# FFN products and sums of squares in two 64-column halves of the array, with a new order table

## The chip, the cores and the metric

The kernel runs on one core of one Trainium2 chip. The metric is the device time of one execution in microseconds (us). TensorE (PE in the profile) multiplies: it holds a block of weights in its array and streams another operand through it into a bank of PSUM. VectorE (DVE), ScalarE (ACT) and GpSimd (POOL) do the elementwise work, and SyncE (SP) issues transfers. Before the change three runs took 1124.65, 1126.27 and 1127.68 us; the median is 1126.27 us.

## The reference

Attention with a threshold below each row's maximum, over 8 batches of 8 heads with 576 positions of 64 elements, and behind it a feed-forward network (FFN) on 4,608 tokens of 512 features with 2,048 hidden ones:

```python
scores = scale * np.matmul(q, k.transpose(0, 1, 3, 2))
thresh = np.max(scores, axis=-1, keepdims=True) - tau
scores = np.where(scores >= thresh, scores, -1000000000.0)
scores = scores - np.max(scores, axis=-1, keepdims=True)
attn = np.exp(scores)
attn = attn / (np.sum(attn, axis=-1, keepdims=True) + 1e-09)
attn_out = np.matmul(attn, v)
...
x = np.ascontiguousarray(attn_out.transpose(0, 2, 1, 3)).reshape(B * S, H * D)
h = x @ w_in
g = np.where(h >= 1, h, np.where(h <= -1, 0.0, (h + 1) ** 2 / 4.0))
return g @ w_out
```

## The kernel before

Every operand of a large product is kept as two float16 parts, a high and a low one, and each product is made of three: high by high, high by low, low by high. Scales are powers of two that come from sums of squares.

The attention is cut by batch, pair of heads and a stretch of 256 or 320 rows (all of batch 0's in pieces of 128, 128 and 320). One *visit* makes two score tiles `s` of 128 rows by 576 (`products`, line 958 of the profile). A head has 64 elements, so these products use 64 of the array's rows, and two of them lie in the two row halves; in a tail visit both rows and columns are halved. A tile then goes through the softmax: VectorE finds the extreme (L1011), ScalarE takes the exponential (L1018), VectorE masks and sums (L1032), GpSimd normalises (L1050), ScalarE and GpSimd split into two parts `hl` (L1055, L1058), and a transposing DMA brings them into `eT`. Then `av` (L1156) multiplies with `v`. It gives 64 columns for each of the two heads of a pair, so it issues two products in turn, one into partitions 0 to 63 of a PSUM bank and one into 64 to 127; each uses 64 of the array's columns. The result becomes `x`, the FFN's input.

The FFN takes tokens in groups of 256 (or 128). `ffn1` (L1225) makes 24 products of 256 columns (48 of 128) into one bank `ph`; ScalarE and VectorE work out the gate (L1231 to L1248) and leave it in `ga`, `gb` or in a freed piece of the weights `WI`, `WO`; `ffn2` (L1270) makes 6 products (or 12) of 512 columns into the one bank `acc`, which ScalarE copies out (`evict`, L1288) when all parts of 128 tokens are in. Up to the change `ffn1`, `ffn2` and the small products with which sums of squares are added over partitions (L546 and L610) all use the whole array of 128 by 128.

So TensorE works in four layouts: the whole array (128*128 in the profile), two column halves (128*64), two row halves (64*128), and both (64*64).

Which engine does what in which order is written down. Each step is an operation of a `Plan`, with the engine, a cost and the buffers it takes. The list `ORDER` gives the sequence in which a planner places the operations; it works out a start time for each by their costs, and the steps are then issued sorted by these. An operation has a `mode` for its layout, and the planner adds `TURN`, 0.097 us, where the mode on TensorE differs from the one before. Small strings choose variants: `CONV` and `SIGN` for the conversion of the weights, `PAIR` for whether a visit's two tiles are one step, `TILE` for a softmax variant, `FSCALE` for the engine that works out a batch's scale factors (L920 to L926). In gaps of the plan's first 200 us, products with `ones` (L1304) keep TensorE active.

Of the kernel before, what the change touches and what calls it, by code (L numbers as in the profile page):

```python
# [18 lines left out]
P = 128  # L19
# [6 lines left out]
CONV = {"i": "GGMGPGGPPPGPMPQP", "o": "QAPADPPAPDPDDADD"}  # L26

SIGN = {"i": "ANANAAANNNNNNANA", "o": "AAANAAAAANAANAAD"}
PAIR = "SSJSJSJJSJSJJJJSSJJJJJJJJJJJJJJJJJJJJJJJJJJJJJJJJJJJJJJJJJJJJJJJJJJJJJJJJJJJJJJJJJJJJJJJJJJJJJJJJJJJJJJJJJJJJJJJJJJJJJJJJJJJJJJJJJJJJJJJJJJJJJJJ"
# [214 lines left out]
]  # L244
ESC = 2.0 ** 15

TILE = {0: "T", 1: "T", 71: "S", 272: "S"}
FSCALE = "GVVGVGGV"
EPS = 1e-9

# [15 lines left out]
class Plan:  # L266
# [38 lines left out]
    def order(self):  # L305
# [5 lines left out]
        for o in (self.ops[n] for n in ORDER):  # L311
# [10 lines left out]
            if o.eng == "PE":  # L322
                mode = o.mode
# [20 lines left out]
def attn_ffn_kernel(ctx: ExitStack, tc: tile.TileContext, qT, kT, vT, tau, w_in, w_out, out):  # L344
# [87 lines left out]
    def ap(b, arr):  # L432
        return arr[b.slot]
# [926 lines left out]
```

## Time and profile before

| | before |
|---|---|
| median of 3 runs (lowest to highest), us | 1126.27 (1124.65 to 1127.68) |
| the profiled execution, us | 1124.36 |
| its span, us | 1122.6 |
| mean granted clock of TensorE | 0.994 |
| HBM read, written | 45.09 MB, 9.44 MB |

The span runs from the first to the last instruction that was profiled. Busy times count an engine's own instructions; a product's row lasts until its result is out, which is longer than the distance to the next one. The distance between two rows' starts in the timeline is therefore the better measure of what a group of products takes.

### The profile page before, as it was taken

The numbers are of one execution on the slowest core, as the hardware profiler recorded it, in microseconds if no ns is written. First come the engines' busy times: TensorE is split into PE (matmuls) and PEld (weight loads), VectorE is DVE, ScalarE is ACT, GpSimd is POOL, SyncE is SP. The second block draws the span as 40 slices with busy tenths as digits, with TensorE's granted clock in tenths as the row PEclk, the third lists the DMA queues.
The fourth block names the chain that finished last, engine by engine and source line by source line (L and its number), as shares of the span: only waits on it lengthen the run. The fifth ranks groups of instructions, "written<-read, shape, count | busy, mean of one in ns | idle before, by whom it ended". The sixth has DMA issues, their size and how long they took to land.

```text
span 1122.6 us, 28192 instructions
## 1 busy us (share of the span) xinstructions
PE 1084.0 (97%) x10251; PEld 731.1 (65%) x10251; DVE 887.5 (79%) x2677; ACT 868.2 (77%) x1675; POOL 789.4 (70%) x912
## 2 busy tenths in 40 slices
PE   8789989999999999999999999999999999999998
PEld 7557647666766666666667666666676666766774
DVE  5899988998888887788879887788788797886331
ACT  7899768798788887788788798678788776776442
POOL 5999998787658986788768886676668885655000
PEclk9899999999999999999999999999999999999999
DMA  9797696868776985678666875757657667546000
GB/s 350 299 248 118 135 190 129 151 127 147 129 144 135 167 178 99 116 143 185 138 112 134 161 151 122 125 100 157 152 119 119 120 122 126 103 100 115 12 20 19
DMA packets 418011, 154.68 MB, mean 138 GB/s; under 512 B 396880, under 2 KB 396880, under 8 KB 417872
## 3 DMA queue, kind: packets, MB, share of 16 engines
q1 hardware_dynamic: 417872, 152.88, 66.7%
q8 instruction: 80, 1.31, 0.5%
q14 instruction: 59, 0.48, 0.2%
HBM read 45.09 MB, written 9.44 MB: 49 GB/s over the span
## 4 chain that ended last, share of the span: by engine, by line
PE 69%; DVE 9%; POOL 9%; ACT 4%; DMA 4%; issue 4%; SPq 0%; POOLq 0%; DVEq 0%; ACTq 0%
PE ph L1225 26%; PE acc L1270 25%; PE ph L1156 8%; PE s L958 8%; DMA eT<-hl 4%; POOL hl L1058 3%; DVE s L1011 2%; POOL e L1050 2%; DVE e L1032 2%; ACT hl L1055 1%; PE ph L1304 1%; ACT e L1018 1%; DVE ph L1238 1%; POOL raw L566 1%; PE s L660 1%
## 5 line engine op out<-in xcount | busy, mean ns | idle before, releaser
L1058 POOL TENSOR_TENSOR hl<-e,hl 128x576 f16<-128x576 f32 x284 | 364.1, 1290 | 91.3 <-ACT hl L1055 86.6
L1225 PE MATMUL ph<-x,WI 128*128 128x256 f16 (+1 forms) x4032 | 401.1, 258 | 2.4 <-DVE x L1168 0.8
L1225 PEld LDWEIGHTS <-WI 128*128 128x128 f16 x4032 | 343.7, 98 | 60.1 <-issue 16.4
L1050 POOL TENSOR_SCALAR e<-e,sm 128x576 f32<-128x576 f32 x284 | 219.9, 779 | 108.7 <-DVE sm L1042 80.4
L1011 DVE TENSOR_SCALAR_CACHE_REDUCE s<-s,pc 128x576 f32<-128x576 f32 x288 | 229.5, 819 | 49.2 <-PE s L958 46.3
L1032 DVE SCALAR_TENSOR_TENSOR e<-s,sm,e 128x578 f32<-128x578 f32 x284 | 229.1, 816 | 42.7 <-ACT e L1018 34.2
L1055 ACT ACTIVATE hl<-e 128x576 f16<-128x576 f32 x284 | 192.1, 681 | 84.2 <-POOL e L1050 67.3
L1018 ACT ACTIVATE e<-s,sm 128x576 f32<-128x576 f32 x288 | 209.6, 739 | 37.9 <-DVE s L1011 27.9
L1270 PE MATMUL acc<-WO,ga 128*128 128x512 f16 x864 | 202.2, 379 | 0.7 <-ACT ob L1288 0.4
L1238 DVE SCALAR_TENSOR_TENSOR ph<-ph,fcs,asq 128x512 f32<-128x512 f32 (+1 forms) x160 | 111.8, 700 | 66.7 <-ACT asq L1234 65.7
L958 PE MATMUL s<-kk,qq 64*128 64x288 f16 (+1 forms) x1920 | 141.5, 285 | 6.9 <-DVE e L1032 4.0
L1231 ACT ACTIVATE asq<-ph,fcs 128x512 f32<-128x512 f32 (+1 forms) x160 | 115.8, 736 | 37.6 <-PE ph L1225 36.1
L1270 PEld LDWEIGHTS <-ga 128*128 128x128 f16 x864 | 80.1, 98 | 93.1 <-issue 10.6
L1156 PE MATMUL ph<-eT,vst 128*64 128x320 f16 (+2 forms) x1928 | 123.3, 280 | 6.2 <-DMA eT<-hl 4.7
L958 PEld LDWEIGHTS <-qq 64*128 64x128 f16 (+1 forms) x1920 | 81.0, 96 | 65.1 <-issue 47.3
L1156 PEld LDWEIGHTS <-vst 128*64 128x64 f16 x1928 | 98.5, 110 | 34.4 <-issue 24.6
L1243 ACT ACTIVATE ga<-ph,fcs 128x256 f16<-128x256 f32 (+1 forms) x160 | 70.2, 450 | 29.6 <-DVE ph L1238 24.4
L1234 ACT ACTIVATE asq<-asq 128x512 f32<-128x512 f32 x144 | 90.5, 630 | 2.0
L1248 DVE SCALAR_TENSOR_TENSOR ga<-ph,fcs,ga 128x256 f16<-128x256 f32 (+1 forms) x160 | 70.9, 452 | 22.2 <-ACT WO L1243 7.4
L1270 PE MATMUL acc<-WO,gb 128*128 128x512 f16 x300 | 71.9, 379 | 0.0
L1270 PE MATMUL acc<-WO,WI 128*128 128x512 f16 x300 | 71.7, 379 | 0.0
L1270 PE MATMUL acc<-WO 128*128 128x512 f16 x264 | 63.4, 379 | 1.9 <-ACT ob L1288 1.9
(186 smaller groups left out, 1136.5 us busy)
## 6 DMA issues: line engine op xcount, KB each, us to landing
raw<-in_v_dram SPq DMA_DIRECT2D x32, 288.0 KB, 3.4
raw<-in_q_dram SPq DMA_DIRECT2D x32, 288.0 KB, 3.5
raw<-in_k_dram SPq DMA_DIRECT2D x32, 288.0 KB, 3.5
WO<-in_moe_w_in_dram SPq DMA_DIRECT2D x16, 512.0 KB, 8.5
out_dram<-ob SPq DMA_DIRECT2D x32, 256.0 KB, 2.5
x<-in_moe_w_out_dram SPq DMA_DIRECT2D x10, 512.0 KB, 6.8
eT<-hl SPq DMA_TRANSPOSE x286, 3.4
WO<-in_moe_w_out_dram SPq DMA_DIRECT2D x4, 512.0 KB, 6.1
```

What stands on the lines that cost most here:

```text
L958: T.matmul(ap(sb, s_ps)[r, f, :SH], ap(qb, qq)[h, ql, c : c + r.stop - r.start], ap(kb, kk)[h, kl, f * SH : (f + 1) * SH], start=ql == kl ...
L1011: V.tensor_scalar(sv(), sv(), c[:, 24 + v : 25 + v], None, ALU.mult, ALU.min, accum_out=t[:, 0:1])
L1018: A.activation(ev(), sv(), AF.Exp, bias=ap(m, sm)[:, 0:1], scale=-1.0)
L1032: V.scalar_tensor_tensor(ev(SH + 1), sv(SH + 1), t[:, 2:3], ev(SH + 1), ALU.is_le, ALU.mult, accum_out=t[:, 3:4])
L1050: G.tensor_scalar(ev(), ev(), ap(m, sm)[:, 5:6], ESC, ALU.mult, ALU.mult)
L1055: A.activation(part2(0), ev(), AF.Copy)
L1058: G.tensor_tensor(part2(w), ev(), part2(0), ALU.subtract)
L1156: T.matmul(o[hd * D : (hd + 1) * D, :n], vt[:, k, hd * D : (hd + 1) * D], t[:, kb, (hd ^ p % 2) * n : ((hd ^ p % 2) + 1) * n], start=m == ...
L1225: T.matmul(h[:, i], WTh["i"][:, u, wl * 512 + c * P : wl * 512 + (c + 1) * P], x[:, cc, xl, c0 : c0 + n].rearrange("p (t n) -> p t n", n=P ...
L1231: A.activation(tv()[:, :, c], hv()[:, :, c], AF.Relu, bias=fcs[:, b, 2, q : q + 1], scale=fcs[:, b, 3, q : q + 1])
L1238: V.scalar_tensor_tensor(hv()[:, :, c], hv()[:, :, c], fcs[:, b, 0, q : q + 1], tv()[:, :, c], ALU.max, ALU.min)
L1270: T.matmul(ap(ab, accs), gv(h, gl)[:, x], WTh["o"][:, fc + i, wl * 512 : (wl + 1) * 512], start=fc + i == 0 and m == 0, stop=not left[0] a ...
```

## The change

A function `columns` issues a product as two products of 64 weight columns each, the first into partitions 0 to 63 of the result and the second into 64 to 127, or as one whole product where `halves` is false. The FFN-1 of groups of 256 tokens, all of FFN-2 and the sums of squares go through it; the FFN-1 of 128 tokens stays whole. Their mode is a new one, 4, which stands for "either". `layouts` walks TensorE's operations in order and decides for each of mode 4: it keeps the layout of the last operation with a mode of its own if that is the whole array or the column halves; behind a layout of row halves it takes that of the next operation with a mode of its own, if that is the whole array or the column halves, and otherwise the column halves. `turned` is the same rule in the planner. The planned costs of the sums of squares are lower.

```diff
-CONV = {"i": "GGMGPGGPPPGPMPQP", "o": "QAPADPPAPDPDDADD"}
-
-SIGN = {"i": "ANANAAANNNNNNANA", "o": "AAANAAAAANAANAAD"}
+CONV = {"i": "GGMGPGGPPPGPMPQP", "o": "PAPADPPAPDPDDADD"}
+
+SIGN = {"i": "ANNNAAANNNNNNANA", "o": "AAANAAAAANAANAAD"}
...
 ORDER = [
-    0, 58, 56, 60, 54, 623, 633, 638, 4, 57, 628, 1, 5, 59, 2, 61, 658, 55, 648, 62, 63, 625, 653, 64, 624, 80, 626, 635, 643, 634, 75, 81, 636, 640,
...
+    0, 54, 58, 59, 56, 57, 60, 623, 633, 638, 1, 4, 628, 5, 2, 55, 658, 61, 648, 653, 625, 643, 62, 63, 64, 900, 80, 624, 626, 627, 634, 75, 635, 636,
...
-TILE = {0: "T", 1: "T", 71: "S", 272: "S"}
-FSCALE = "GVVGVGGV"
+TILE = {0: "T", 1: "T", 71: "S", 214: "S", 287: "S"}
+FSCALE = "GVGGGGGV"
...
+    def turned(self, at, to):
+
+        if to == 4:
+            return (False, at) if at in (0, 1, 4) else (True, 4)
+        return at != to and not (at == 4 and to < 2), to
+
+    def layouts(self, order):
+
+        at, after = 0, {}
+        seq = [o for o in order if o.eng == "PE"]
+        for o in reversed(seq):
+            after[o.n] = at
+            if o.mode != 4:
+                at = o.mode
+        at = 0
+        for o in seq:
+            if o.mode != 4:
+                at = o.mode
+            elif at > 1:
+                at = after[o.n] if after[o.n] < 2 else 1
+            o.layout = at
...
+    def columns(out, lhsT, rhs, halves=True, **flags):
+
+        for x in (slice(0, D), slice(D, P)) if halves else (slice(0, P),):
+            T.matmul(out[x], lhsT[:, x], rhs, **flags)
...
-                T.matmul(o[:, 2 * v : 2 * v + 2], sel[:, 2 + p % 2 if v == 2 else v], c, start=True, stop=True)
-
-        ps = plan.op("PE", 0.25, sums, [sq, sk], take=[sb], uses=[cb])
+                columns(o[:, 2 * v : 2 * v + 2], sel[:, 2 + p % 2 if v == 2 else v], c, ps.layout, start=True, stop=True)
+
+        ps = plan.op("PE", 0.18 if b else 0.09, sums, [sq, sk], take=[sb], uses=[cb], mode=4)
...
-                            T.matmul(h[:, i], WTh["i"][:, u, wl * 512 + c * P : wl * 512 + (c + 1) * P],
-                                     x[:, cc, xl, c0 : c0 + n].rearrange("p (t n) -> p t n", n=P), start=m == 0, stop=m == 3 * NCC - 1)
+                            columns(h[:, i], WTh["i"][:, u, wl * 512 + c * P : wl * 512 + (c + 1) * P],
+                                    x[:, cc, xl, c0 : c0 + n].rearrange("p (t n) -> p t n", n=P), k == 2 and me[0].layout, start=m == 0, stop=m == 3 * NCC - 1)
...
-                            T.matmul(ap(ab, accs), gv(h, gl)[:, x], WTh["o"][:, fc + i, wl * 512 : (wl + 1) * 512],
-                                     start=fc + i == 0 and m == 0, stop=not left[0] and i == k - 1 and m == 2)
+                            columns(ap(ab, accs), gv(h, gl)[:, x], WTh["o"][:, fc + i, wl * 512 : (wl + 1) * 512], me[0].layout,
+                                    start=fc + i == 0 and m == 0, stop=not left[0] and i == k - 1 and m == 2)
```

How this moves instructions is seen best on TensorE. In its built order before, around the end of an attention step a little before the middle of the program (`vst` is `v`, `eT` the transposed weights of attention; the last number is partitions by columns of the result):

```order
L1156 LDWEIGHTS vst_85
L1156 MATMUL ph_65<-eT_97,vst_85 64x256
L1225 LDWEIGHTS WI
L1225 MATMUL ph_64<-x_104,WI 128x2x128
L1225 LDWEIGHTS WI
L1225 MATMUL ph_64<-x_104,WI 128x2x128
```

And after, the start of the same attention step on TensorE, with what stands ahead of it:

```order
L461 LDWEIGHTS WI
L461 MATMUL ph_63<-x_104,WI 64x2x128
L461 LDWEIGHTS WI
L461 MATMUL ph_63<-x_104,WI 64x2x128
L1184 LDWEIGHTS vst_85
L1184 MATMUL ph_65<-eT_97,vst_85 64x256
```

Before, the step comes from scores and goes on to FFN-1 in the whole array; after, FFN-1 in halves of 64 columns stands ahead of it, and FFN-2 in halves behind it. Every half is an instruction of its own with its own weight load: TensorE's program has 29,250 rows where it had 20,346.

The second place, on TensorE, is where `acc` passes from one block of 128 tokens to the next, near 487 us of the profile before. In the order before (`ga` and `WO` hold gates, `sel` and `pc` are those of the sums of squares):

```order
L1270 LDWEIGHTS ga_108
L1270 MATMUL acc<-WO,ga_108 128x512
L546 LDWEIGHTS sel
L546 MATMUL ph_64<-pc_118,sel 128x2
L546 LDWEIGHTS sel
L546 MATMUL ph_64<-pc_118,sel 128x2
L546 LDWEIGHTS sel
L546 MATMUL ph_64<-pc_118,sel 128x2
L1270 LDWEIGHTS WO
L1270 MATMUL acc<-WO 128x512
```

And after, the same passing on TensorE, from the last product of the old block on:

```order
L461 LDWEIGHTS ga_108
L461 MATMUL acc<-WO,ga_108 64x512
L1184 LDWEIGHTS vst_87
L1184 MATMUL ph_63<-eT_96,vst_87 64x320
L1184 LDWEIGHTS vst_87
L1184 MATMUL ph_63<-eT_96,vst_87 64x320
```

Before, three small products lie between the last product into `acc` and the first of the next block; after, the 28 products of an attention step lie there.

The third place is ScalarE at the same passing, before (L1288 copies `acc` out):

```order
L1234 ACTIVATE asq_99<-asq_99 128x512
L1055 ACTIVATE hl_94<-e_92 128x576
L1288 ACTIVATE ob_100<-acc,scs 128x512
L1018 ACTIVATE e_91<-s_62,sm_120 128x2x288
L572 ACTIVATE kk_79<-raw_75 128x576
```

And ScalarE there after (L1321 is the same copy):

```order
L1083 ACTIVATE hl_94<-e_90 128x576
L1262 ACTIVATE asq_98<-asq_98 128x512
L1046 ACTIVATE e_91<-s_62,sm_121 128x2x288
L1321 ACTIVATE ob_100<-acc,scs 128x512
L1046 ACTIVATE e_92<-s_61,sm_122 128x2x288
```

The copy now stands behind an exponential as well, and the rest is exchanged among neighbours.

More of the change, by code (lines that the diff above doesn't have):

```diff
@@ L24 @@
 WIDE = 1
-CONV = {"i": "GGMGPGGPPPGPMPQP", "o": "QAPADPPAPDPDDADD"}
-SIGN = {"i": "ANANAAANNNNNNANA", "o": "AAANAAAAANAANAAD"}
-PAIR = "SSJSJSJJSJSJJJJSSJJJJJJJJJJJJJJJJJJJJJJJJJJJJJJJJJJJJJJJJJJJJJJJJJJJJJJJJJJJJJJJJJJJJJJJJJJJJJJJJJJJJJJJJJJJJJJJJJJJJJJJJJJJJJJJJJJJJJJJJJJJJJJJ"
+CONV = {"i": "GGMGPGGPPPGPMPQP", "o": "PAPADPPAPDPDDADD"}
+SIGN = {"i": "ANNNAAANNNNNNANA", "o": "AAANAAAAANAANAAD"}
+PAIR = "JSJSSSJJSJSJSJJSJJJJJJJJJJJJJJJJJJJJJJJJJJJJJJJJJJJJJJJJJJJJJJJJJJJJJJJJJJJJJJJJJJJJJJJJJJJJJJJJJJJJJJJJJJJJJJJJJJJJJJJJJJJJJJJJJJJJJJJJJJJJJJJJ"
 QHOW = "DDPDPPDPPPDPPPPPPPPPPPPPPDDPPPPP"
@@ L320, in order @@
                 b.since = t
-            end = idle[o.eng] = t + o.cost + (self.TURN if o.eng == "PE" and o.mode != mode else 0.0)
+            end = idle[o.eng] = t + o.cost
             if o.eng == "PE":
-                mode = o.mode
+                turn, mode = self.turned(mode, o.mode)
+                end = idle[o.eng] = end + self.TURN * turn
             if o.work:
@@ L609, in sums @@
         def sums():
-            T.matmul(stat(sb.slot, NPAIR), ones, cut(vssq[:, b, :]), start=True, stop=True)
-        ps = plan.op("PE", 0.1, sums, squares + [c_op], take=[sb])
+            columns(stat(sb.slot, NPAIR), ones, cut(vssq[:, b, :]), ps.layout, start=True, stop=True)
+        ps = plan.op("PE", 0.06 if b else 0.03, sums, squares + [c_op], take=[sb], mode=4)
         s = scs[:, b, :]
@@ L1214, in gv, with ffn1 @@
                 return (ga, gb)[h][qs[h].slot].rearrange("p (l k n) -> p l k n", l=2, n=P)[:, l]
-            def ffn1(hv=hv, g=g, fc=fc, c0=c0, n=n, k=k, q=q):
+            def ffn1(me, hv=hv, g=g, fc=fc, c0=c0, n=n, k=k, q=q):
                 h = hv().rearrange("p (t k) n -> p k t n", k=k)
@@ L1251, in attn_ffn_kernel @@
             wo = [wlo["o", x] for x in range(fc, fc + k)]
-            o = plan.op("PE", 12 * k * (n / 2400 + 0.0027), ffn1, xdone[g, c0] + xdone.get((g, c0 + n - P), []) + wi, take=[hb, qs[1]], uses=[xbuf[g]])
+            me = []
+            o = plan.op("PE", 12 * k * (n / 2400 + 0.0027), partial(ffn1, me), xdone[g, c0] + xdone.get((g, c0 + n - P), []) + wi, take=[hb, qs[1]], uses=[xbuf[g]],
+                        mode=4 if k == 2 else 0)
+            me.append(o)
             o = plan.op("ACT", 0.7 + 0.295 * (m - 1), relu, [o] + [fscale[b] for b in bs], take=[tb], uses=[hb])
@@ L1263, in attn_ffn_kernel, with ffn2 @@
             for fc, qs, gv, need in steps:
-                def ffn2(gv=gv, ab=ab, fc=fc, t0=t0, k=k, left=left):
+                def ffn2(me, gv=gv, ab=ab, fc=fc, t0=t0, k=k, left=left):
                     left[0] -= 1
@@ L1269, in ffn2 @@
                         for gl, wl in ((0, 0), (0, 1), (1, 0)):
-                            T.matmul(ap(ab, accs), gv(h, gl)[:, x], WTh["o"][:, fc + i, wl * 512 : (wl + 1) * 512],
-                                     start=fc + i == 0 and m == 0, stop=not left[0] and i == k - 1 and m == 2)
+                            columns(ap(ab, accs), gv(h, gl)[:, x], WTh["o"][:, fc + i, wl * 512 : (wl + 1) * 512], me[0].layout,
+                                    start=fc + i == 0 and m == 0, stop=not left[0] and i == k - 1 and m == 2)
                             m += 1
-                o.append(plan.op("PE", 3 * k * 0.216, ffn2, need, take=[ab] if fc == 0 else [], uses=[*(qs if k == 4 else [qs[t0 // P]]), ab], behind=head))
+                me = []
+                o.append(plan.op("PE", 3 * k * 0.216, partial(ffn2, me), need, take=[ab] if fc == 0 else [], uses=[*(qs if k == 4 else [qs[t0 // P]]), ab], behind=head, mode=4))
+                me.append(o[-1])
                 head = o[0]
@@ L1324, in attn_ffn_kernel @@
         order = plan.order()
+        plan.layouts(order)
         left = gaps(order)
```

406 rows, old and new, of the table ORDER are left out of this document.

## The prediction

> **What bounds the kernel now.** I read the page first, then the table of stretches, then TensorE's timeline. The page's engine rows (busy time, share, instructions) and its chain of work, followed back from the end:
>
> ```profile
> PE 1084.0 (97%) x10251; PEld 731.1 (65%) x10251; DVE 887.5 (79%) x2677; ACT 868.2 (77%) x1675; POOL 789.4 (70%) x912
> ...
> PE 69%; DVE 9%; POOL 9%; ACT 4%; DMA 4%; issue 4%; SPq 0%; POOLq 0%; DVEq 0%; ACTq 0%
> ```
>
> TensorE is busy 97% and carries 69% of the chain. The table of stretches says where the other 3% lie (length, then busy time of PE, PEld, DVE, ACT and POOL, the granted clock, the DMA share, GB/s):
>
> ```profile
> 0.00:100.00 100.00, 81.97 (x1015) 63.09 (x1016) 81.12 (x263) 88.22 (x174) 82.04 (x144) 0.95 0.89 272
> 100.00:200.00 100.00, 92.53 (x940) 61.55 (x938) 90.20 (x266) 78.69 (x151) 91.42 (x98) 1.00 0.80 149
> 200.00:500.00 300.00, 294.81 (x2735) 196.99 (x2735) 253.62 (x773) 244.51 (x477) 228.65 (x252) 0.99 0.74 139
> 500.00:800.00 300.00, 299.64 (x2769) 200.95 (x2768) 248.65 (x747) 239.70 (x462) 224.08 (x248) 1.00 0.70 138
> ```
>
> The first 200 us leave 25.5 us idle; from 500 to 800 the idle time is 0.36 us. So after the start the time is the sum of what TensorE executes, and a nanosecond saved there is a nanosecond of the end. But "busy" hides something, which the timeline shows by the distance from start to start (start, busy time, instructions):
>
> ```profile
> 611.73 0.91 PE L958 MATMUL s<-kk,qq 64*128 64x288 f16 x12
> 612.57 1.47 PE L1270 MATMUL acc<-WO 128*128 128x512 f16 x6
> 613.88 1.46 PE L1270 MATMUL acc<-WO,gb 128*128 128x512 f16 x6
> 615.17 0.22 PE L546 MATMUL ph<-pc,sel 128*128 128x2 bf16 x3
> 615.25 2.78 PE L1225 MATMUL ph<-x,WI 128*128 128x256 f16 x24
> 617.87 2.75 PE L1270 MATMUL acc<-WO,gb 128*128 128x512 f16 x12
> 620.46 1.46 PE L1270 MATMUL acc<-WO,WI 128*128 128x512 f16 x6
> 621.85 0.91 PE L958 MATMUL s<-kk,qq 64*128 64x288 f16 x12
> 622.69 2.76 PE L1270 MATMUL acc<-WO,WI 128*128 128x512 f16 x12
> 625.38 2.09 PE L1156 MATMUL ph<-eT,vst 128*64 128x320 f16 x28
> 627.40 0.93 PE L958 MATMUL s<-kk,qq 64*64 64x288 f16 x24
> 628.27 1.47 PE L1270 MATMUL acc<-WO,ga 128*128 128x512 f16 x6
> 629.57 1.46 PE L1270 MATMUL acc<-WO,WI 128*128 128x512 f16 x6
> ```
>
> Twelve FFN-2 products followed by more of their own shape take 617.87 to 620.46, 2.59 us; twelve followed by attention products in the 128*64 shape take 622.69 to 625.38, 2.69. Six take 1.29 before sums (613.88) and 1.39 before scores (620.46). Each change of layout (the shape behind the tile names) costs 0.095 us or so, with no wait in it.
>
> **Part 1, the changes of layout.** Walking TensorE's built order and counting the places where the layout of neighbouring products differs gives 374 before and 323 after. The 298 that enter or leave a layout of 64 rows (scores) stay 298: halves have 128 rows, and a score visit still lies between two changes. Those between whole array and 64 columns fall from 76 to 25: 51 x 0.095 = **-4.85 us**. All of it is on the path, since TensorE waits for nothing there.
>
> The entry into a layout has a small cost of its own. Two groups give it, and give the pace of half-width products too:
>
> ```profile
> 601.30 1.72 PE L1156 MATMUL ph<-eT,vst 128*64 128x256 f16 x28
> 602.95 1.47 PE L1270 MATMUL acc<-WO,ga 128*128 128x512 f16 x6
> ...
> 834.47 3.25 PE L1156 MATMUL ph<-eT,vst 128*64 128x256 f16 x56
> ...
> 1044.56 8.02 PE L1225 MATMUL ph<-x,WI 128*128 128x256 f16 x72
> ...
> 1055.01 2.78 PE L1225 MATMUL ph<-x,WI 128*128 128x256 f16 x24
> ```
>
> The 28 half-width products above stand 1.65 us until the next group; less 0.095 and less 14 pairs at 0.1093 (below) 0.025 is left for the entry. Into the whole array it is 0.01 (612.57 to 613.88 is 1.31 for six products, where 1.30 is usual). Stretches of half-width work rise from 65 to 137, those of whole-array work fall from 161 to 38: 72 x 0.025 - 123 x 0.01 = **+0.6 us**.
>
> **Part 2, 8,760 half-width FFN products in place of 4,380 whole ones.** 2,880 FFN-1 products of 256 columns and 1,500 of the 1,728 FFN-2 products are issued as two halves of 64 columns, one behind the other, into the two halves of one bank. Attention already works so, and the four rows above give its pace: 28 more products take 3.25 - 1.72 = 1.53 us, so a pair takes 109.3 ns; 48 more whole products take 8.02 - 2.78 = 5.24 us, 109.2 each. A pair of halves costs what one whole product costs: **0 us**. The 512-column pair isn't in the trace; at 320 columns a group of 28 stands 2.02 us (625.38 to 627.40), less 0.095 and 0.025 is 136 ns a pair, and 320/512 of FFN-2's 216 ns (2.59 us / 12) is 135. The other end: if the 0.025 of an entry were spread over its 14 pairs, each pair would carry 1.8 ns, 4,380 x 1.8 = +7.9 us. I take 0, since the longer row decides between the two readings, and keep +7.9 for the range. The whole gain of part 1 is 1.0 ns a pair; nothing below 0 is to be had, as the columns streamed stay the same.
>
> Each half needs its own weight load. The page has for the two kinds:
>
> ```profile
> L1225 PEld LDWEIGHTS <-WI 128*128 128x128 f16 x4032 | 343.7, 98 | 60.1 <-issue 16.4
> ...
> L1156 PEld LDWEIGHTS <-vst 128*64 128x64 f16 x1928 | 98.5, 110 | 34.4 <-issue 24.6
> ```
>
> A half load takes 110 ns, a whole one 98, and yet the pair above keeps 109.3: loads go on behind products. The Trainium skill, "TensorEngine Tiling (Array Packing)", Restrictions, says that column tiling switches fast weight load off, a rule against this change; the trace agrees that half a load isn't shorter (110 against 98), and not that it shows in the pace. By the rule alone, with loads in the open, the sum would end far above the time before (third rival).
>
> **Part 3, sums of squares (L546, L610).** 26 of the 32 groups of three tiny products become six halves. Three take 0.08 us (615.17 to 615.25). If halves run side by side as attention's do, nothing is added; one after the other, 26 x 0.08 = +2.1 us. Nearest is attention's row: **0**, the other end kept.
>
> **Part 4, the new order.** It mostly keeps the neighbourhoods; work on the other engines is the same but for a few conversions. One wait is visibly taken on. TensorE and ScalarE around it:
>
> ```profile
> 484.82 2.76 PE L1270 MATMUL acc<-WO,ga 128*128 128x512 f16 x12
> 487.42 0.22 PE L546 MATMUL ph<-pc,sel 128*128 128x2 bf16 x3
> 489.55 1.46 PE L1270 MATMUL acc<-WO 128*128 128x512 f16 x6 [1.91 <-ACT ob L1288]
> 490.93 2.09 PE L1156 MATMUL ph<-eT,vst 128*64 128x320 f16 x28
> 492.96 0.91 PE L958 MATMUL s<-kk,qq 64*128 64x288 f16 x12
> ...
> 487.73 0.62 ACT L1234 ACTIVATE asq<-asq 128x512 f32<-128x512 f32 x1
> 488.25 0.67 ACT L1055 ACTIVATE hl<-e 128x576 f16<-128x576 f32 x1
> 488.82 0.68 ACT L1288 ACTIVATE ob<-acc,scs 128x512 f32<-128x512 f32 x1
> ```
>
> The one accumulator must be copied out (L1288) before the next tokens' FFN-2 may start, and the copy stands behind two activations. TensorE has 0.08 us of sums to fill 2.13 us. In the new order attention's 28 products (2.03 us, 490.93 to 492.96) stand there instead: **-1.9 us**. What is late next: if the copy is later still, 0.1 us or so. Elsewhere a handover gets narrower: one near 220 us has 1.1 us of TensorE work between where it had 2.6. A copy takes 0.68 plus its queue; I set +0.3 (0 to +1.0). Two of the four small chains of scale factors that VectorE worked out go to GpSimd. It is busy 70%, and no row has TensorE waiting for these: 0.
>
> All waits of TensorE after 200 us, of which I count no others as gone (ten rows, 8.2 us together):
>
> ```profile
> PE ph L1156 <- DMA eT<-hl: 2.2, 2, 1.6
> PE acc L1270 <- ACT ob L1288: 1.9, 1, 1.9
> PE s L958 <- DVE e L1032: 1.5, 4, 0.5
> ...
> PE ph L1156 <- issue: 0.3, 1, 0.3
> ...
> PE ph L1225 <- DVE gb L1248: 0.2, 1, 0.2
> ```
>
> **Sum:** -4.85 + 0.6 + 0 + 0 - 1.9 + 0.3 = **-5.9 us**. The profiled execution took 1124.36 us (span 1122.6 and 1.8 around it): 1118.5. It lies 1.9 us below the median of the runs, 1126.27, from which the sum gives 1120.4. I take the middle, **1119.4**.
>
> **Rivals.**
> *New waits eat it.* The order was dealt anew, and a step that was just in time may be late. For it: softmax steps hold two score buffers, and VectorE is 85% busy from 200 to 500 (253.62 of 300). Against it: the neighbourhoods barely differ. Three waits of the size of the longest DMA wait, 1.6 us, make +4.8: 1124, the same within measurement.
> *The halves don't save the change.* If going from an FFN half to an attention half costs as much as a change of layout, only parts 1's +0.6 and part 4 remain: 1124.3. Against it: inside attention's rows the two halves alternate at full pace.
> *Loads in the open.* Here the price starts at 12 ns a pair (110 - 98): 4,380 x 12 = 53 us, 1172. Only the 56-product row, whose halves have different moving data, speaks against it; FFN halves share theirs. It decides from 1.0 ns a pair on.
> *The instruction stream, slower.* TensorE's program grows from 20,346 rows to 29,250. The queues of the page:
>
> ```profile
> q1 hardware_dynamic: 417872, 152.88, 66.7%
> q8 instruction: 80, 1.31, 0.5%
> ```
>
> 1.31 MB over 2 x 10,251 is 64 bytes each: q8 feeds TensorE, and gets 115 packets where it had 80, beside traffic that keeps the DMA engines 67% busy. If packets come late by the 0.3 us of the one "issue" wait, 31 of them undo 5.9 us and put the kernel 0.3% above; at 75 late ones +22.5: 1142. Place: stretches of FFN-1 halves, four instructions in 109 ns. Against it: attention runs at this rate, if only for 3 us at a time.
>
> **How the numbers follow.** A measurement of this kernel tells about 0.3% (3.4 us) from no change: below 1122.9 is faster, above 1129.6 slower. My forecast with the smaller mishaps has 0.64; new waits 0.24, a twelfth of it beyond 1129.6; halves that save nothing 0.04; the stream 0.06; open loads 0.02. Faster 0.64; same 0.22 + 0.04 = 0.26; slower 0.02 + 0.06 + 0.02 = 0.10. The range reaches down to 1112, where half of the remaining waits (3 us) and a sixth of the first 200 us' idle time go too, and up to 1128, which takes in part 2's +7.9 (1127.3) and the new waits.
>
> **What would show it.** FFN-1 groups in halves with 2.62 us from start to start for 24 pairs, and 1.30 for six FFN-2 pairs, show part 2 right; 2.67 or more shows the surcharge. FFN halves followed by attention without 0.09 us extra show part 1. The wait for L1288's successor near 485 us should be gone. "issue" in TensorE's waits beyond 1 us would show the stream. I am wrong if the waits after 200 us exceed 11 us, or if the first 200 us get longer by 3.

## The result, and the profile after

| | before | after |
|---|---|---|
| median (lowest to highest), us | 1125.46 (1122.65 to 1127.68), 4 runs | 1112.17 (1111.71 to 1114.32), 4 runs |
| the profiled execution, us | 1124.36 | 1114.32 |
| its span, us; granted clock | 1122.6; 0.994 | 1112.5; 0.991 |

The changed kernel takes 0.9887 of the time of the kernel before (95% interval 0.986 to 0.9913): 13.3 us less, where 5.9 were forecast from the sum (6.9 from the median then shown). The sign is right, the size half of what came, and the time is just inside the range's lower end.

The page after, engine rows (busy time, share of the span, instructions) and the chain by engine:

```profile
PE 1080.0 (97%) x14703; PEld 793.3 (71%) x14703; DVE 898.6 (81%) x2668; ACT 871.3 (78%) x1675; POOL 789.5 (71%) x921
...
PE 77%; DVE 8%; ACT 4%; DMA 4%; POOL 3%; issue 2%; SPq 0%; DVEq 0%; ACTq 0%; POOLq 0%
```

TensorE still carries the chain, with 77% of it instead of 69%. It was busy for 4.0 us less, while the span shrank by 10.1: most of what came is idle time. Stretches of the changed kernel (length, then busy time of PE, PEld, DVE, ACT and POOL, granted clock, DMA share, GB/s):

```profile
0.00:100.00 100.00, 81.67 (x951) 62.09 (x952) 79.16 (x257) 84.29 (x168) 79.19 (x143) 0.91 0.90 269
100.00:200.00 100.00, 95.45 (x1258) 68.95 (x1259) 93.56 (x274) 81.71 (x155) 94.14 (x102) 1.00 0.81 150
200.00:500.00 300.00, 297.45 (x4233) 220.62 (x4227) 260.32 (x779) 252.57 (x488) 235.84 (x264) 1.00 0.79 142
500.00:800.00 300.00, 297.60 (x4154) 217.62 (x4148) 252.40 (x745) 240.34 (x460) 219.94 (x244) 1.00 0.75 139
```

The first 200 us leave 22.9 us idle (25.5 before). TensorE's timeline (start, busy time) shows the halves:

```profile
608.60 2.79 PE L461 MATMUL ph<-x,WI 128*64 128x256 f16 x48
611.22 1.46 PE L461 MATMUL acc<-WO,WI 128*64 128x512 f16 x12
612.52 1.46 PE L461 MATMUL acc<-WO 128*64 128x512 f16 x12
613.81 1.46 PE L461 MATMUL acc<-WO,gb 128*64 128x512 f16 x12
615.21 1.21 PE L986 MATMUL s<-kk,qq 64*128 64x288 f16 x12
...
1029.92 2.07 PE L1184 MATMUL ph<-eT,vst 128*64 128x320 f16 x28
1031.82 2.76 PE L461 MATMUL acc<-WO,ga 128*64 128x512 f16 x24
```

From start to start, 24 pairs of FFN-1 take 2.62 us and six of FFN-2 1.30 or 1.29, and the six ahead of scores 1.40, one change of layout more. Attention's 28 products pass into FFN-2 in halves after 1.90 us; into the whole array it was 2.02. Both are as forecast, so the missing 7 us lie elsewhere.

TensorE's waits after 200 us show where to look: what waited, for whom, total us, times, longest. The kernel before in a second profiled execution (`e8_before_again` below):

```profile
PE ph L1156 <- DMA eT<-hl: 2.7, 2, 1.4
PE acc L1270 <- ACT ob L1288: 1.8, 1, 1.8
PE s L958 <- DVE e L1032: 1.3, 3, 0.5
PE ph L546 <- DVE pc L553: 0.7, 1, 0.7
```

and the changed kernel:

```profile
PE ph L1184 <- DMA eT<-hl: 2.7, 4, 1.0
PE ph L1184 <- DVE e L1060: 1.6, 1, 1.6
PE ph L1184 <- issue: 0.4, 1, 0.4
PE ph L461 <- DVE WI L1276: 0.2, 1, 0.2
```

In the kernel before the longest waits come back in both executions at the same places, at 417, 487 and 868 us, 8.2 and 7.7 us in all; they belong to its order. After, the accumulator's handover (the row with `ob`) and the score products' wait for masked tiles (`s` for `e`) are gone; 4.9 us are left.

### The profile page after: what moved, and what is told of

The parts are those of the page before. It is cut to its first block, busy times and chain, and to the rows that moved or that the text cites. A ratio compares the mean times of both kernels' runs of the same rounds, so it can differ in the third digit from the quotient of the medians.

```text
span 1112.5 us, 37005 instructions
## 1 busy us (share of the span) xinstructions
PE 1080.0 (97%) x14703; PEld 793.3 (71%) x14703; DVE 898.6 (81%) x2668; ACT 871.3 (78%) x1675; POOL 789.5 (71%) x921
## 3 DMA queue, kind: packets, MB, share of 16 engines
q1 hardware_dynamic: 417872, 152.88, 70.9%
## 4 chain that ended last, share of the span: by engine, by line
PE 77%; DVE 8%; ACT 4%; DMA 4%; POOL 3%; issue 2%; SPq 0%; DVEq 0%; ACTq 0%; POOLq 0%
PE ph L461 30%; PE acc L461 28%; PE s L986 9%; PE ph L1184 8%; DMA eT<-hl 3%; DVE s L1039 2%; DVE e L1060 1%; POOL hl L1086 1%; ACT hl L1083 1%; PE ph L1337 1%; ACT e L1046 1%; POOL e L1078 1%; DMA raw<-in_k_dram 0%; DMA WO<-in_moe_w_in_dram 0%; DVE sm L1043 0%
## 5 line engine op out<-in xcount | busy, mean ns | idle before, releaser
L461 PEld LDWEIGHTS <-WI 128*64 128x64 f16 (+1 forms) x7458 | 408.0, 108 | 52.1 <-issue 15.1
L461 PE MATMUL ph<-x,WI 128*64 128x256 f16 (+1 forms) x6912 | 400.5, 264 | 0.3 <-DVE WI L1276 0.2
L461 PE MATMUL acc<-WO,ga 128*64 128x512 f16 (+1 forms) x1596 | 203.3, 380 | 0.0
L461 PEld LDWEIGHTS <-ga 128*64 128x64 f16 (+1 forms) x1596 | 92.5, 109 | 80.7 <-issue 9.0
L461 PE MATMUL acc<-WO,gb 128*64 128x512 f16 (+1 forms) x576 | 73.9, 380 | 0.0
L461 PE MATMUL acc<-WO,WI 128*64 128x512 f16 (+1 forms) x546 | 69.9, 380 | 0.0
L461 PE MATMUL acc<-WO 128*64 128x512 f16 (+1 forms) x510 | 64.5, 380 | 0.0
```

The lines of the kernel that those rows point to most:

```text
L461: T.matmul(out[x], lhsT[:, x], rhs, **flags)
```

## The experiments

Ratios are to the kernel before, run on the same chip beside the experiment, with 95% intervals.

### The order without the halves, the halves without the order

Is it the order or the halves? `e1_new_order_whole` is the changed kernel with `columns` always whole, so "the order" takes in the strings (`PAIR` differs as well) and the planned costs that came with the new table:

```diff
-        for x in (slice(0, D), slice(D, P)) if halves else (slice(0, P),):
+        for x in (slice(0, P),):
```

> The changed kernel with every product whole again (the function that issues halves issues one product of 128 columns); the new order table stays, and with it the order on every engine. TensorE's order then has 387 changes of layout instead of 323. If the gain is the layouts' alone (theory L), it is gone: 1124 to 1126 us. If the layouts give 0.095 us a change and the order gives the rest by shorter waits (theory O), 64 x 0.095 less 0.7 for entries comes back: 1112.2 + 5.4 = 1117.6 us, and TensorE's waits after 200 us stay near 5 us.

`e2_old_order_halves` is the kernel before, old order and all, with the same rule for the layout put onto its FFN products and sums:

```diff
+    def layouts(self, order):
...
+            elif at > 1:
+                at = after[o.n] if after[o.n] < 2 else 1
+            o.layout = at
...
+                            columns(ap(ab, accs), gv(h, gl)[:, x], WTh["o"][:, fc + i, wl * 512 : (wl + 1) * 512], me[0].layout,
```

> The kernel before with its own order table and the same rule for halves: FFN-1 of 256 tokens, FFN-2 and sums of squares take the layout of their neighbours. 325 changes of layout instead of 374. Theory L: nearly the whole gain, 1112 to 1114 us. Theory O: 49 x 0.095 less 0.6 for entries, 4.1 us off 1125.5: 1121.4 us, with waits after 200 us still near 8 us or more.

`e3_all_halves` is the changed kernel with the FFN-1 of 128 tokens in halves as well:

```diff
-                                    x[:, cc, xl, c0 : c0 + n].rearrange("p (t n) -> p t n", n=P), k == 2 and me[0].layout, start=m == 0, stop=m == 3 * NCC - 1)
+                                    x[:, cc, xl, c0 : c0 + n].rearrange("p (t n) -> p t n", n=P), me[0].layout, start=m == 0, stop=m == 3 * NCC - 1)
...
-                        mode=4 if k == 2 else 0)
+                        mode=4 if k == 2 else 0, either=True)
...
```

> The changed kernel with the FFN-1 of 128 tokens in halves too (1,152 more products of 128 columns as pairs). 317 changes of layout instead of 323: both theories 0.6 us less by the changes. If pairs of 128 columns keep the 56 ns of one whole product, 1111.6 us; if a pair of that size costs 2 ns more, 2.3 us come back: 1114 us.

`e4_after_again` is the changed kernel, unchanged, for the same chip.

> The changed kernel unchanged, to see what one execution's waits are worth: if the waits after 200 us are drawn anew in each execution, their list changes in its places and its sum (4.9 us before) by 1 to 2 us; if they are set by the order, the same places come again within 0.3 us. Time 1112.2 us either way.

| | changes of layout | median, us | ratio |
|---|---|---|---|
| the kernel before | 374 | 1122.93 | 1 |
| e1: new order, whole products | 387 | 1113.59 | 0.9914 (0.9899 to 0.993) |
| e2: old order, halves | 325 | 1125.85 | 1.0025 (1.0014 to 1.0036) |
| e3: new order, all in halves | 317 | 1115.76 | 0.9934 (0.9915 to 0.9954) |
| e4: the changed kernel | 323 | 1111.35 | 0.9895 (0.988 to 0.9911) |

The order alone brings 9.3 us, with 13 changes of layout more than before. The halves alone, with 49 fewer, cost 2.9. On the new order they bring 2.2 by the medians, for 64 changes fewer, and the intervals of e1 and e4 overlap. With the FFN-1 of 128 tokens in halves as well (e3) the kernel is 0.4% slower than e4. The price of these pairs isn't the reason: in e3's trace a group of 48 stands 2.692 us until the next, where 48 whole products stand 2.685. e3's profiled execution, 1113.31 us, is the fastest of its six, so its trace doesn't show what the others lost; the cause stays open.

The waits of e1:

```profile
PE ph L1184 <- DMA eT<-hl: 1.0, 2, 0.6
PE ph L1184 <- DVE e L1060: 0.7, 1, 0.7
PE ph L1184 <- DVE ph L1266: 0.7, 1, 0.7
PE ph L461 <- DVE WI L1276: 0.2, 1, 0.2
```

and of e2, its longest four:

```profile
PE s L980 <- DVE e L1054: 5.0, 9, 1.3
PE ph L1178 <- DMA eT<-hl: 2.3, 4, 1.3
PE ph L1178 <- DVE sm L1064: 1.7, 2, 1.5
PE acc L455 <- ACT ob L1314: 1.4, 1, 1.4
```

The new order with whole products waits 2.6 us after the first 200, the old one with halves 12.1. TensorE saved its changes there and then stood waiting, most of all for the softmax (the first three of these rows).

### The waits that the prediction named, taken alone

Does a single place carry the gain? Part 4 had named two: the scale chains given to GpSimd, and the accumulator's handover. `e5_old_order_scales_on_pool` gives the old order the new assignment, and `e7_new_order_scales_on_dve` the new order the old one, by the reverse edit:

```diff
-FSCALE = "GVVGVGGV"
+FSCALE = "GVGGGGGV"
```

> The kernel before with the new string for the scale factors alone: those of batches 2 and 4 are worked out by GpSimd and not by VectorE. If the order's 9 us come from a few named places (theory N), VectorE's 2.3 us near 486 us go, the 2.05 us wait behind them shrinks, and the kernel gains 1 to 2.5 us: about 1121. If the gain lies in the order as a whole (theory B), 0 to -0.5 us: 1122.5 to 1123.

> The changed kernel with the old string for the scale factors: VectorE works out those of batches 2, 3 and... of every batch that it had before (1, 2, 4, 7), GpSimd the others. Theory N: 1 to 2.5 us more, 1113 to 1114. Theory B: the slack of the order takes it, 1111.3 to 1112.

`e6_old_order_attention_moved` moves one step in the old list, the attention products that the new order has at the handover (2262), ahead of the first FFN-2 of the next tokens (4292):

```diff
-    ..., 2282, 334, 2287, 4292, 2295, 2286, ..., 335, 2283, 340, 2262, 4311, 337, ...
+    ..., 2282, 334, 2287, 2262, 4292, 2295, 2286, ..., 335, 2283, 340, 4311, 337, ...
```

> The kernel before with one entry of its order table moved: the attention step behind the 487 us handover of the accumulator stands ahead of the next block's first FFN-2 products instead of behind them. Nothing else moves. One more change of layout, +0.1; the handover's wait of 1.9 us is filled. Theory N: 1.8 us less, 1121.1. If the softmax, and not TensorE, sets the pace there, the 1.8 us turn up as a wait of the next scores: 1122.9.

`e8_before_again` is the kernel before, profiled beside them (1123.01 us).

> The kernel before unchanged, for a second trace. If TensorE's waits after 200 us are set by the order, the same places come again, and near 8.2 us; if each execution draws its own, half of the places are others and the sum is anywhere from 5 to 12 us.

Beside a median of 1123.02 before, e5 took 1126.11 us, 1.0021 (1.0008 to 1.0034); e6 1123.14, 0.9991 (0.9977 to 1.0004); e7 1112.23, 0.9901 (0.9885 to 0.9917). The chains cost a little on the old order (in e5's trace the handover's wait is 3.1 us, not less than before), their return costs nothing that can be told on the new one, and moving the attention step isn't to be told from no change, although it takes the handover's wait away. TensorE's timeline of e6 at that place:

```profile
486.69 0.22 PE L546 MATMUL ph<-pc,sel 128*128 128x2 bf16 x3
488.57 2.09 PE L1156 MATMUL ph<-eT,vst 128*64 128x320 f16 x28 [1.66 <-DVE pc L553]
490.59 1.47 PE L1270 MATMUL acc<-WO 128*128 128x512 f16 x6
```

The attention products stand ahead of the accumulator's next block, as in the new order, but now they wait 1.66 us themselves, for VectorE's work on the sums (`pc`). One wait was exchanged for another of the same size. In the built order of e6 the sums and the attention products write the same bank, `ph_64`, so attention has to wait until VectorE has read the sums out; in the new order the same attention products write `ph_63` (as printed ahead of the prediction). So the move alone doesn't do it; the steps around it have to fit.

### How much lateness an order bears

If the new order gains by leaving more room around each handover, it should bear steps that come late better. `e11_old_order_late_exps` (from the kernel before) and `e12_new_order_whole_late_exps` (from e1) do a tile's exponential twice, 28 times over the run, some 17 us more of ScalarE's busy time (867.8 in e8, 885.1 in e11):

```diff
-            A.activation(ev(), sv(), AF.Exp, bias=ap(m, sm)[:, 0:1], scale=-1.0)
+            for _ in range(2 if j >= 64 and (37 * j + 11) % 8 == 0 else 1):
+                A.activation(ev(), sv(), AF.Exp, bias=ap(m, sm)[:, 0:1], scale=-1.0)
```

> The kernel before with lateness put in: in every eighth softmax tile from the 65th on (28 tiles) ScalarE takes the exponential twice, some 0.65 us later each time; the result is the same. If the old order has little slack for a late step (theory B), TensorE takes on a third or more of the 18 us: 1123 + 6 to 12 = 1129 to 1135 us. If both orders have the same slack, it adds the same to both (next run).

> The new order with whole products (1113.6 us) and the same 28 repeated exponentials. Theory B: the new order absorbs most of it, +0 to 4 us: 1114 to 1118. If the new order is only better fitted to the durations as they are, it loses as much as the old one, 6 to 12 us: 1120 to 1126.

Beside 1121.67 us before, e11 took 1132.63, 1.0095 (1.0075 to 1.0115), and e12 1115.01, 0.9945 (0.9926 to 0.9965). The same lateness costs the old order 0.95%, about 11 us, and the new one 0.31% over e1's 0.9914, about 3.5 (0.06 to 0.56% by the two intervals, as e1 ran on another chip; the two profiled executions differ by 1.0 us). Two rows of e11's waits after 200 us:

```profile
PE s L958 <- DVE e L1033: 3.7, 8, 0.8
PE ph L1157 <- DMA eT<-hl: 3.4, 4, 1.4
```

and e12's two longest:

```profile
PE ph L1185 <- DVE sm L1071: 1.0, 1, 1.0
PE ph L1185 <- DMA eT<-hl: 0.5, 1, 0.5
```

The old order hands the lateness on to TensorE, in the softmax's own handovers above all (11.6 us of idle time after 200 us, 8.3 in e8), and the new one takes it in (2.4, 2.7 in e1). Idle time is only a part of it: of the 12.1 us between the spans of e11 and e8, 6.3 are TensorE's busy time (1092.4 against 1086.1), 1.7 of them by one more stretch of half clock (see part 4 below).

### Halves in one of the two FFN products

What does a change of layout cost on the new order? `e9_new_order_ffn1_halves` keeps FFN-2 whole, `e10_new_order_ffn2_halves` FFN-1, the order being that of the changed kernel, so that neighbours differ more often. The edit of e9 is shown; that of e10 puts the same `False` into FFN-1:

```diff
-                            columns(ap(ab, accs), gv(h, gl)[:, x], WTh["o"][:, fc + i, wl * 512 : (wl + 1) * 512], me[0].layout,
+                            columns(ap(ab, accs), gv(h, gl)[:, x], WTh["o"][:, fc + i, wl * 512 : (wl + 1) * 512], False,
```

> The changed kernel with halves for FFN-1 of 256 tokens alone; FFN-2 is whole. 485 changes of layout, so the time only says that they cost: 1113.6 + 98 x 0.095 = 1123 us. It is run for the transposing DMAs, whose mean time to landing after 200 us was 3.58 to 3.60 us in five traces with whole products and 3.76 to 3.82 in five with halves. If the added instructions slow them (2 x 2,880 of the 2 x 4,380 added, 66%), the mean is 3.59 + 0.66 x 0.19 = 3.72; if the second reading of the moving operand does (737,000 of 1,505,000 columns, 49%), 3.68; if it is neither but the higher rate of TensorE, 3.59.

> The changed kernel with halves for FFN-2 (and sums of squares) alone; FFN-1 is whole. 436 changes, 1113.6 + 49 x 0.095 = 1118 us. Mean landing of the transposes: by the added instructions (34%) 3.65 us, by the columns read twice (51%) 3.69.

Beside 1121.67 us before, e9 (485 changes) took 1127.41, 1.0049 (1.003 to 1.0068), and e10 (436) 1119.92, 0.9976 (0.9964 to 0.9987). Over e1's 387 these are 98 and 49 changes more, for 15.2 and 7.0 us by the ratios: 0.155 and 0.143 us each (0.13 to 0.18 and 0.10 to 0.19 by the intervals, with what the entries and the halves themselves cost). So a change isn't cheaper than the 0.095 of the prediction; what the halves take away in changes they give back in part elsewhere.

## Why the prediction was right in sign and half of the size

**What bounds it: right.** Every experiment moved the time through TensorE, by what it executes or by what it waits for.

**Part 1, the changes: mechanism right, worth less than its price.** The changed kernel's trace has 323 changes, each 0.09 to 0.10 us, and attention passes into halves without one. What the term left out stands in parts 2 and 3.

**Part 2, pairs at 0: nearly.** Means of the distance from start to start over all groups after 200 us that are followed by their own layout without a wait (number of groups):

| us | before | e1 | after | e2 |
|---|---|---|---|---|
| FFN-1, 24 products or pairs | 2.6262 (50) | 2.6265 (33) | 2.6337 (43) | 2.6346 (52) |
| FFN-2, six | 1.2991 (98) | 1.2997 (104) | 1.3042 (113) | 1.3042 (111) |
| sums, three | 0.0799 (18) | 0.0798 (18) | 0.0936 (18) | 0.0924 (16) |

A pair of FFN-1 costs 0.3 to 0.4 ns more than a whole product, a pair of FFN-2 0.8 to 0.9. Over 120 groups and 250 that is 0.9 + 1.3 us, after against before. Single rows, read to 10 ns, can't decide what 4,380 pairs sum up to; the mean over the groups can. The Trainium skill, "TensorEngine Tiling (Array Packing)", Restrictions, has column tiling without fast weight load: a half load took 108 ns in the changed kernel against 98 for a whole one in the kernel before, and next to nothing of it shows in the pace. The rival of loads in the open, with 12 ns a pair, is out.

**Part 3, sums at 0: nearly.** 26 groups with 0.014 us more each: 0.4 us.

The halves on the new order then come to 64 x -0.095 = -6.1, +0.4 of entries (71 stretches of half-width work more, 135 of whole-array work fewer), and about +2.5: -3.2. Waits after 200 us went up by 0.4 to 2.3 us (2.6 in e1; 3.0 and 4.9 in two executions of the changed kernel). Measured: -2.2. On the old order, 49 x -0.095 = -4.7, +0.6 and +2.5 make -1.6, and waits grew by 4.4 (7.7 to 12.1): +2.8. Measured: +2.9. An account that fits both: rid of changes, TensorE comes sooner to a handover whose other side comes no sooner. The sums rest on one or two traces each.

**Part 4, the new order at -1.6 (-1.9 and +0.3): this is the step that failed.** It reads: "All waits of TensorE after 200 us, of which I count no others as gone (ten rows, 8.2 us together)". The wait near 487 us went, as forecast. But the order alone brought 9.3 us, and in spite of 13 changes more, where the term had 1.6. From the second execution of the kernel before to e1 the span falls by 9.2 us (1121.2 to 1112.0). TensorE's idle time after 200 us falls from 8.3 to 2.7 us, -5.6; the first 200 us are alike (22.1 and 22.3). The second piece is the clock. TensorE's timeline before, at the waits near 417 us:

```profile
416.90 0.23 PE L546 MATMUL ph<-pc,sel 128*128 128x2 bf16 x3 [0.52 <-DVE pc L553]
417.63 0.28 PE L958 MATMUL s<-kk,qq 64*128 64x288 f16 x1 [0.50 <-DVE e L1032]
418.37 0.89 PE L958 MATMUL s<-kk,qq 64*128 64x288 f16 x11 [0.46 <-DVE e L1032]
419.19 7.08 PE L1225 MATMUL ph<-x,WI 128*128 128x256 f16 x48
426.11 1.46 PE L1270 MATMUL acc<-WO,ga 128*128 128x512 f16 x6
```

48 products take 6.92 us from start to start, where twice 2.62 is usual: 1.7 us lost with no wait in it. The stretches behind them (length, busy time, granted clock, DMA share, GB/s) say why:

```profile
420.00:421.00 1.00, 1.00 (x6) 0.50 1.12 211
421.00:422.00 1.00, 1.00 (x7) 0.50 1.07 209
...
424.00:425.00 1.00, 1.00 (x11) 1.00 0.08 28
```

Both profiled executions of the kernel before have this stretch of half clock; neither e1 nor the changed kernel has any between 75 and 1100 us. The second execution has another between 150 and 160 us (mean clock 0.83 over 10 us), which isn't counted here: the FFN-2 group that started at 158.20 us in the first execution started at 159.84, but the wait behind it then was 0.54 us instead of 1.55, and the FFN-1 group at 199.90 us in the first started at 199.21. Nor does the new order run at a higher clock as a whole: before 75 us e1 has 20.5 us of half clock, the two executions of the kernel before 10.2 and 13.7. The other runs on record say the same: the 57 executions of the kernel before that ran beside experiments have a mean granted clock of 0.9925, e1's six 0.9917, and the five of the 57 with the highest, 0.995, still have a mean span of 1119.8 us, 7.7 above e1's 1112.1 (all 57: 9.2 above).

So -5.6 of waits, -1.7 of clock and +1.4 of changes (13 x 0.095, and 0.15 for their entries) make -5.9 of the 9.2. Two smaller pieces show in the traces. Idle time understates a wait, because the row ahead lasts beyond the moment when the next could have started (0.08 us of sums fill 2.13 us near 487 us, of which 1.91 count as idle): from start to start e8's eleven waits of over 0.15 us cost 9.3 us where 7.7 are idle, e1's five 3.3 where 2.7 are, which makes 1.0 us more. And at 200 us e1 has eleven products of FFN-1 more behind it (355 against 344 of 256 columns), 1.2 us, with the other large products equal. The rest, 1.1 us, I can't assign. The prediction valued one wait at its length, without the clock that can follow a wait, and left the other nine rows of waits standing; half of them going it had kept for the lower end of the range, 1112, just under the measured time. None of its own signs of being wrong came, since they looked for new waits and not for old ones that go.

**The rivals.** New waits did not eat the gain: 4.9 us after 200 against 8.2. On the old order they did (e2), where the prediction hadn't looked for it. The halves do save the change (1.90 us against 2.02 behind attention). The longer instruction stream stayed harmless, "issue" making one wait of 0.4 us; its queue in the page after:

```profile
q8 instruction: 115, 1.88, 0.7%
```

**What is shown and what isn't.** Shown: the order, with the strings that came with it, brings the greater part (e1), neither of the two named places alone does (e5, e6, e7), the new order takes in lateness at about a third of the cost (e11, e12), and halves without the order lose (e2). Only argued: the shares of waits, clock and head start in the order's 9.2 us, since they are read from one execution of e1 and two of the kernel before. Not tried: the strings other than `FSCALE` taken alone, and a version of the old order with all its waits taken away and the rest kept. No experiment was faster than the changed kernel.

## What to carry to other kernels

On a kernel that one engine bounds to 97%, repeat the profile: waits that return at the same places belong to the order, and a new order is to be valued by all of them, and by the stretch of lower clock that may follow one, not by the one wait that can be followed by eye. Work saved on the bounding engine is paid out only where its suppliers have room; test that by making a step late on purpose, which cost one order 11 us here and the other 3.5. Taking one wait away by moving one step may only move the wait, as it did here.

## What the runs showed of the hardware

**Half the clock after short waits, but not each time.** The stretch of half clock near 420 us lasts 3.4 us and follows three waits that are 1.5 us together. In e6 the same three waits lead to none:

```profile
417.70 0.23 PE L546 MATMUL ph<-pc,sel 128*128 128x2 bf16 x3 [0.71 <-DVE pc L553]
418.43 0.28 PE L958 MATMUL s<-kk,qq 64*128 64x288 f16 x1 [0.50 <-DVE e L1032]
419.17 0.89 PE L958 MATMUL s<-kk,qq 64*128 64x288 f16 x11 [0.46 <-DVE e L1032]
419.99 5.42 PE L1225 MATMUL ph<-x,WI 128*128 128x256 f16 x48
425.24 1.46 PE L1270 MATMUL acc<-WO,ga 128*128 128x512 f16 x6
```

5.25 us for the 48 products, at full clock. The longer single waits of the kernel before, 1.91 us near 487 and 1.60 near 868, are followed by none; in e5 a wait of 3.08 us near 490 is followed by 3.4 us of half clock. The Trainium skill, "TensorE: Matmul & The Clock Gate", Part 1, describes a free-running window of about 3.4 us, and half the clock after at least one idle window. The length of the stretch, 3.4 us, agrees, and so does that it comes in one execution and not in another; that a whole window must be idle doesn't, as in the two executions of the kernel before 1.5 and 1.6 us of waits with small products between them were enough.

**With halves in both FFN products the transposing DMAs take longer.** The queue that moves the data, and the transposes of the attention weights (issues, median us from issue to landing), before:

```profile
q1 hardware_dynamic: 417872, 152.88, 66.7%
...
eT<-hl SPq DMA_TRANSPOSE x286, 3.4
```

and after, with the same packets and bytes:

```profile
q1 hardware_dynamic: 417872, 152.88, 70.9%
...
eT<-hl SPq DMA_TRANSPOSE x286, 3.5
```

The queue's share is 65.7 to 67.2% in the seven profiles with whole products alone, 69.2 in e2, and 70.9 to 71.5 in the four executions with halves in the new order (after, e3, e4, e7). With halves in one FFN product it is 68.0 (e9) and 67.6 (e10), less than in proportion. The mean from issue to landing of a transpose after 200 us, for which e9 and e10 were run, is 3.63 and 3.60 us, close to the 3.57 to 3.61 of the seven with whole products and below both forecasts by proportion (3.72 and 3.68; 3.65 and 3.69); with halves in both it is 3.76 to 3.82. The higher rate of TensorE can't be the cause alone, as e2 has 3.76 at a span of 1124.7 us. The cause stays open. Halves in both products lengthen a transposed tile's way to TensorE by 0.1 us in the median (0.2 in e3), which may be part of why the waits for `eT` came back with the halves.
